# Batch 0 of a fused attention and feed-forward kernel: two of three head groups over all queries at once, undivided plain columns, and a finer first cast

## The chip, the cores and the metric

The kernel runs on one core of a Trainium2 chip. The metric is the device time of one execution in microseconds (us), the median of the runs shown. The engines are named as in the profile: PE (TensorE, the matrix unit; PEld its weight loads), ACT (ScalarE), DVE (VectorE), POOL (GpSimd, which here issues most loads), SP (SyncE, which issues stores and the transposing loads).

## The reference

Two stages follow one another: attention with a squared ReLU in place of softmax, and a feed-forward pair with an exact GELU.

```python
scores = scale * np.matmul(q, k.transpose(0, 1, 3, 2))   # q, k, v: (8, 12, 448, 64) float32
attn = np.maximum(scores, 0.0) ** 2 / S
attn_out = np.matmul(attn, v)
x = attn_out.transpose(0, 2, 1, 3).reshape(B * S, H * D) # (3584, 768)
h = x @ w_in                                             # w_in: (768, 2048)
g = 0.5 * h * (1.0 + erf(h * inv_sqrt2))
return g @ w_out                                         # w_out: (2048, 768)
```

## The kernel before

All products run in bfloat16. There are eight batches; a batch has three head groups of four heads (G = 3), and 448 keys in seven blocks of 64 (NK = 7).

**Attention.** For one head group, `add_tk` and `add_tq` turn k and q on PE (tiles `tp`) and copy them out to `kT` and `qT`; from batch 2 on, transposing loads do this instead. `add_steps` makes one *step* out of one or two key blocks: the scores on PE into a PSUM tile `ps` (line 806), the scaled ReLU on ACT or DVE into a tile `a_sq` (lines 823, 825), the square on DVE or ACT (lines 835, 833). A step with all 448 queries holds one key block; where queries come in two halves of 224, a step holds two blocks of one half, so that both kinds give `a_sq` the same 896 columns. `add_av` multiplies the seven squared blocks with v (tile `pav`, line 885) and two copies put the result into `xT`, the input of the feed-forward stage (lines 548 and 550, which serve every copy and cast).

In batch 0 before the change, all three groups are cut into halves of queries: `halves(0)` takes the seven blocks of group 0, half 0, then the rest, half 1 last. Batches 1 to 7 take all queries at once, by `steps(b)`.

**Feed-forward.** Of the first layer's sixteen columns of 128 features, batch 0 computes eight directly: `add_f1`, tile `psh`, line 947, with a GELU on ACT (line 957). These are called plain columns here. They need `xT` of all three head groups. Before the change each plain `psh` tile holds two feature columns over half of the queries; the tiles of half 0 come first, so they need no attention of half 1. All else in the first layer, and the second layer, uses a seven-product block scheme (Winograd's), with tiles `pe` and `pb` (lines 1103, 1256) for the first layer and `pso` (line 1432) for the second.

**Order.** Nothing is scheduled at run time. Every operation is an `Op` in a list; the table `ORDER` names them one by one with their engine (P and Q for PE, where Q takes the other kind of PSUM bank; A for ACT, D for DVE, G for POOL, S for SP; Z is a filler matmul), and the instructions of each engine are issued in that order. `HOMES` gives each tile its buffer: "w" three PSUM tiles of two banks, "f" two of one bank, "a" fourteen `a_sq` buffers. An engine works strictly down its list: what waits holds up all that stands behind it on that engine.

**The start.** The first parts of k and q (tiles `k32`, `q32`; group 0) come as float32 by loads on ACT and SP, and are cast by `early`; all other loads are issued by POOL, in their order, with at most eight under way. Nine matmuls on zeros (`spin`) run ahead of the first transposes. The cast of k is cut at `K_CUT` = 4 blocks of seven; q32 holds the first two of four chunks of q.

Of the kernel before, what the change touches and what calls it, by code (L numbers as in the profile page):

```python
# [12 lines left out]
B, H, S, D = 8, 12, 448, 64  # L13
# [71 lines left out]
0120120120120121210210210201201201201201201201202012010021210011021201201201021012102021021200221121  # L85
2201201201200120210210202020010212002102102102102121011001121010201012012012012010110011220112012012
021211000101201210212012021
""".replace("\n", ""),
    "f": """
0101010101010101011010101011010101010101011011010101010010101010101010101010101010101001010100110101  # L90
01010
""".replace("\n", ""),
    "a": """
0123456789abcd32105649c8b297301a546d89c723b14605ada8c91734526d0a918b652c74301abd98c6b2a50419d3879483
d174725ac60b893d271064ba53c893c210a74d3a89a37405628bc14d29a8564db03718078313d710b52a8c49670532d20985
7b137987357398a06c14d2a7359b57b259aa760814cd39b264513c807ba
# [3 lines left out]
D16 G3 G2 Q17 D18 A13 P14 D15 A19 Q20 D21 P22 D23 P45 D46 P42 A43 P39 G4 G7 P24 A40 D25 P32 D33 P36  # L100
D37 P57 A58 Z1024 Q51 A52 Q28 D41 D29 D44 Q34 D35 D59 A47 G10 Q30 A31 P54 A55 G6 P26 D27 P99 P84 A85
Z672 P69 A70 Q72 D38 D53 D56 P60 A61 D100 D62 D71 A73 G5 P48 A49 P66 D50 A67 D68 P114 A115 Q87 A88
G121 P78 A79 D116 D74 P96 D97 G8 P63 A64 G9 Q75 A65 A76 A77 P93 D94 P111 P105 A106 D112 D113 D80
D107 A95 G11 P144 A145 P108 A109 P81 A82 A83 G120 Q132 P134 D133 G12 P146 A147 D135 P167 A168 P161
A162 D86 D89 D110 P179 D180 D98 D101 P148 A149 P90 A91 D92 G129 P173 A174 D169 G125 G124 Q136 D137
Q164 A165 P102 A103 A104 D175 P117 D118 A119 P170 D171 D172 D253 P138 A139 D163 D166 D181 D254 P176
A177 D178 P245 A246 P194 A195 P185 A186 D187 P200 G123 G128 A201 P150 A151 P249 A250 P197 D198 D199
P188 A189 P191 A192 P142 P140 P203 A204 D141 G122 P182 D143 P209 A210 A183 D205 D193 D196 P215 A216
A184 P247 A248 P251 A252 P212 A213 P221 A222 G127 G126 D190 D202 P206 A207 A208 Q224 G131 P261 P278
D257 D258 P218 A279 D255 D225 A262 A219 G152 G153 Q227 A228 P268 P285 A269 D256 P264 P281 D214 A282  # L110
A265 P263 P280 D223 A211 D217 D259 P273 D260 P270 P287 G130 A220 D226 D229 D266 D286 D288 A289 Q230
A231 A232 D271 P276 P293 D283 D274 A277 A294 D374 P290 D375 D377 P378 D291 P395 A396 A379 P380 P385
P402 A275 A386 A403 A284 D376 D412 D415 P397 D400 D383 A272 P381 P398 D413 A382 P407 A399 D408 P416
P433 D434 A401 P404 P390 G240 G241 D450 P387 D391 A292 A384 D388 D405 A417 A392 A409 P419 P436 A437
A389 P423 P440 A420 A441 D414 G243 D453 D457 P410 A267 D458 P393 A411 A394 S233 P425 P442 D443 S234
Q302 A424 D426 P314 A315 A427 A303 P445 P428 P431 D429 A430 P418 D446 D451 D459 A432 Q308 A309 A444
P317 A318 P435 D438 D421 D454 P448 A449 D456 D460 D319 P462 A463 P305 A306 P311 P320 A321 A322 P464
A316 D465 P466 P468 D452 D304 D461 G155 G156 G158 G159 G239 A312 A467 S236 S235 P329 A406 A330 A313
P341 A342 D469 D455 P335 D336 D310 D307 A439 P470 D471 P472 P326 D327 S238 A447 A422 D494 S237 P368
A369 P350 A351 D495 P474 D475 P362 G242 G154 P323 G157 G160 A363 D473 D324 P344 D328 D352 A345 D346  # L120
A325 A337 D331 D496 P353 A354 D355 D497 P498 A499 P500 D501 P338 A339 D340 D343 P359 P332 A333 D334
G244 G295 G296 G297 S478 S476 A364 A360 A370 P502 D503 P504 D505 P356 A361 P347 A348 A349 D357 A358
P365 D366 D367 P506 D507 S479 P532 P523 A524 P526 D527 A533 P508 P514 D515 D516 D525 P520 A521 P371
A372 A373 D586 P529 P517 A518 A530 P510 D528 P590 A522 P607 A608 D587 D589 P597 D511 D531 P592 P614
A615 D591 D588 P609 D595 A596 G298 P593 P619 D612 P610 P626 A598 D624 P602 A611 D620 A594 P643 A627
A534 A644 G299 G300 G484 S481 S482 S483 S477 A613 D603 A604 A621 P616 P599 D617 D600 A601 P628 P645
D648 D631 D509 A618 P629 A632 D630 P622 D625 P605 P633 P650 D651 A623 A606 P646 P635 A634 S480 P547
Q538 A539 D676 A548 P655 P638 D636 D647 D519 D639 A640 P641 P652 P556 D656 A657 A557 D653 P544 D545
G487 G301 Q535 G490 G485 G486 D536 P568 G488 G489 G491 G492 A642 A654 P541 A542 D677 P658 A659 D540
D537 P680 D681 A569 A549 D678 D543 S662 D570 P565 D566 S512 P574 A575 P553 A554 A555 P682 P684 D683  # L130
A685 P550 A551 S660 S513 P562 P577 A563 A578 A649 A637 S663 S661 G666 G669 P686 D546 D558 D552 P688
D687 D689 P580 D581 P571 G493 P559 A572 A576 A560 P716 P734 A735 A561 P690 D679 P692 D579 D717 D696
D697 A567 A564 A718 D691 D699 D693 S695 P728 P722 A729 P719 A720 A723 P700 D701 P702 D721 D573 A582
P704 P740 A741 D703 P731 D732 D705 A724 P583 A584 A585 P749 D750 A736 P725 A726 A727 P708 P792 P809
D698 P794 P706 P811 D788 D733 D751 D742 D789 P799 P816 A817 A810 D730 D707 D709 P712 A793 D800 P710
D814 D791 P795 A796 D713 A815 D797 A798 P804 D711 P821 D805 P812 D813 P752 D822 A753 Q737 P743 A744
P755 A756 A757 D790 P801 P818 D819 P828 P845 A829 A823 A846 A738 A739 P830 D802 P824 P847 D826 D827
P831 P848 D850 D833 A851 A803 D832 D849 S665 S664 Q764 G672 G667 G668 G670 P835 P852 P837 P854 G671
G673 G674 A825 A806 A765 A745 P807 A808 D836 D853 D838 D855 A856 P840 P857 D841 A839 A842 D878 D858
D879 D880 P843 P860 A844 A861 P882 A859 A883 P746 A747 P773 P770 D771 D772 D766 S715 S862 S714 S864  # L140
S865 P884 D885 A774 D775 P758 S866 S863 P933 P930 A931 D754 P886 D887 A748 D934 G868 G871 G675 P888
P890 D889 D881 A834 A820 A759 D898 D891 P892 D893 S896 P927 D928 D929 P779 A935 A760 A780 D781 P761
A762 A763 P782 D783 P767 D900 D899 P902 A903 P894 D895 D932 A768 D769 A784 P776 A777 P924 D925 D926
P954 A955 A778 S867 S694 G874 G869 G870 P906 P904 D905 P936 D937 P918 A919 G872 G873 G875 A938 G876
P785 D786 D787 P921 A922 D901 P948 P908 A907 P945 A946 D992 D909 A923 P960 A956 A961 A949 P910 D911
D990 P912 P914 D920 D913 D991 D915 P994 A995 D950 P942 A943 A944 Q966 D967 P939 P957 A958 Q951 P1011
D993 P997 S1067 P1001 P1018 A1002 A1019 S916 S1065 G1070 G1073 S1064 S1066 S897 G877 D940 D941 D998
P996 D1012 P1013 D1016 D999 A1000 P1014 D1015 P1023 P1006 D1007 P1030 P1047 P1003 A1008 A968 D1024
A1025 P1032 D1048 P1049 D1028 D1052 A1031 A959 D1035 A1036 P1020 D1021 P1033 P1050 A1051 A1034 A1017
D1004 D1029 D952 D953 P1037 P1054 P1026 A1053 A1055 P1039 P1056 A1038 D1040 D1057 P1009 A1010 A1058  # L150
A1027 P1042 P1059 A1005 D1043 D1060 P1045 P1062 A1046 A1063 A1044 A1041 P1084 A1085 D1080 P969 P978
A979 D1082 P984 A985 D1081 P1086 D970 P1088 D1083 D1087 P1090 A962 A1061 A947 D1091 P972 P1138 A1139
A1022 D973 D974 D971 A986 P963 A1089 A980 P1135 A1136 P975 D964 D976 D965 P1094 D1095 P1092 D1093
P981 A982 P1144 A1145 P1126 A1127 D1100 D1101 D1137 D983 P1104 P1096 D1097 S1099 P1153 D1154 A977
P1159 A1160 P987 A988 A989 P1123 D1124 P1150 A1151 P1106 D1105 P1132 A1133 P1120 A1121 P1129 D1130
P1108 D1107 S917 D1122 D1152 D1102 D1103 D1109 D1161 A1140 A1134 A1155 P1196 P1198 P1215 P1213 A1197
D1201 A1214 P1110 S1069 G1076 S1068 S1098 G1071 G1072 P1112 D1111 D1218 A1219 D1113 A1125 D1192
D1193 P1114 G1074 G1075 G1077 D1115 D1131 D1194 A1128 P1116 D1117 P1162 A1163 D1146 P1141 A1142
D1195 P1168 D1169 Q1147 A1148 A1149 A1143 P1199 P1216 D1170 G1078 S1271 D1200 P1203 P1220 Q1186
D1217 P1156 A1204 A1221 A1187 A1157 P1222 P1205 D1230 D1164 D1206 A1202 D1223 A1224 P1225 P1208  # L160
D1209 A1210 D1226 P1232 P1249 D1250 P1228 D1231 P1234 P1251 A1233 A1188 D1237 D1254 P1235 P1252
A1229 D1253 P1211 P1239 P1256 A1227 A1238 A1255 A1212 D1236 P1241 P1258 D1240 D1242 A1158 A1207
A1257 D1259 A1243 P1180 D1181 A1260 Q1174 A1175 P1244 P1261 P1247 D1262 A1263 P1264 A1265 A1248
# [1607 lines left out]
```

## Time and profile before

| | |
|---|---|
| median of 3 runs | 357.82 us (357.68 to 358.1) |
| profiled execution | 357.81 us, its span 356.0 us |
| granted PE clock | 1.000 |
| busy: PE, ACT, DVE, POOL | 98%, 76%, 86%, 29% of the span |
| matmuls | 3853 |

The span runs from the first to the last instruction of the execution; 1.8 us of its time lie outside. A row of the timeline reads: start, duration, engine, line, operation, output and input, shape, count, and in brackets the idle time ahead of it on that engine and what ended it. Consecutive instructions of one kind stand in one row, and its shape is that of the first of them. Durations overlap at their ends: what an instruction costs its engine's queue is the distance from its start to the next one's.

### The profile page before, as it was taken

How to read it: one execution, taken by the hardware profiler on the slowest of the kernel's cores; microseconds unless marked ns; L12 is line 12 of the kernel's file. 1: busy time of each engine (PE TensorE's matmuls, PEld its weight loads, DVE VectorE, ACT ScalarE, POOL GpSimd, SP SyncE). 2: the span in 40 equal slices, each digit the busy share in tenths (PEclk: the TensorE clock that was granted, in tenths of full speed). 3: DMA queues.
4: the chain of work that ended last, by engine and by line, in shares of the span. 5: the costliest groups of instructions: out<-in, count | busy, mean ns of one | idle time of the engine just before them, and what ended most of it. 6: DMA issues, size and time to landing. Idle time of an engine off the chain costs nothing.

```text
span 356.0 us, 9239 instructions
## 1 busy us (share of the span) xinstructions
PE 348.8 (98%) x3853; PEld 249.7 (70%) x3853; DVE 305.4 (86%) x514; ACT 269.0 (76%) x442; POOL 103.3 (29%) x138
## 2 busy tenths in 40 slices
PE   8899999999999999999999999999999999999995
PEld 4577689855589556786557965669669856888663
DVE  4999999999989998779988979898998799588662
ACT  4999987999978999498787798879986896412500
POOL 8665814195346102901093100290001000000000
PEclk9999999999999999999999999999999999999999
DMA  9999999999999956997699900799309103020222
GB/s 172 200 203 204 184 184 183 162 153 149 200 154 113 184 79 98 124 181 94 132 117 176 175 2 0 186 119 168 37 2 182 22 0 129 8 89 2 88 90 88
DMA packets 123465, 43.01 MB, mean 121 GB/s; under 512 B 100896, under 2 KB 120096, under 8 KB 123424
## 3 DMA queue, kind: packets, MB, share of 16 engines
q0 software_dynamic: 84432, 22.47, 66.9%
q1 hardware_dynamic: 38448, 19.50, 26.0%
q8 instruction: 30, 0.49, 0.6%
q10 hardware_dynamic: 544, 0.46, 0.4%
q14 instruction: 11, 0.09, 0.1%
HBM read 45.61 MB, written 11.01 MB: 159 GB/s over the span
## 4 chain that ended last, share of the span: by engine, by line
PE 93%; ACT 4%; DMA 1%; DVE 1%; issue 0%; DVEq 0%
PE pso L1432 37%; PE pe L1103 30%; PE ps L806 10%; PE pav L885 9%; PE pb L1256 5%; ACT a_sq L823 3%; PE psh L947 2%; DMA k<-in_k_dram 1%; ACT a_sq L833 1%; PE tp L667 0%; PE tp L696 0%; ACT h_sb L957 0%; DVE kT L548 0%; DVE nk L548 0%; ACT xT L550 0%
## 5 line engine op out<-in xcount | busy, mean ns | idle before, releaser
L823 ACT ACTIVATE a_sq<-ps 128x896 bf16<-128x896 f32 (+1 forms) x135 | 108.3, 863 | 9.7 <-PE ps L806 9.6
L1432 PEld LDWEIGHTS <-s_sb 128*128 128x128 bf16 x456 | 43.0, 98 | 31.5 <-issue 4.3
L835 DVE TENSOR_TENSOR a_sq<-a_sq 128x896 bf16<-128x896 bf16 x106 | 61.7, 617 | 1.7 <-ACT a_sq L823 1.0
L1103 PEld LDWEIGHTS <-win_sb 128*128 128x128 bf16 x624 | 59.2, 98 | 3.7 <-issue 2.8
L833 ACT ACTIVATE a_sq<-a_sq 128x896 bf16<-128x896 bf16 (+1 forms) x63 | 58.2, 950 | 0.9 <-DVE a_sq L825 0.6
L825 DVE TENSOR_SCALAR a_sq<-ps 128x896 bf16<-128x896 f32 (+1 forms) x51 | 50.6, 1003 | 3.4 <-PE ps L806 2.8
L1141 DVE TENSOR_TENSOR part<-pe,part 128x448 f32<-128x448 f32 x78 | 45.3, 619 | 8.0 <-PE pe L1103 7.3
L806 PE MATMUL ps<-qT,kT 64*64 64x448 bf16 (+1 forms) x756 | 49.1, 337 | 1.2 <-ACT a_sq L823 0.6
L1153 ACT ACTIVATE h_sb<-part 128x448 bf16<-128x448 f32 x78 | 42.6, 579 | 8.4 <-DVE part L1141 7.9
L1432 PEld LDWEIGHTS <-h_sb 128*128 128x128 bf16 x336 | 31.7, 98 | 23.4 <-issue 4.8
L1103 PEld LDWEIGHTS <-ws 128*128 128x128 bf16 x468 | 44.5, 98 | 2.1 <-issue 1.1
L1432 PE MATMUL pso<-wout_sb,h_sb 128*128 128x384 bf16 x224 | 41.1, 326 | 0.0
L1432 PE MATMUL pso<-t_sb,s_sb 128*128 128x384 bf16 x224 | 41.1, 326 | 0.0
L1432 PE MATMUL pso<-wout_sb,s_sb 128*128 128x384 bf16 (+2 forms) x232 | 41.0, 321 | 0.0
L588 POOL DMA_DIRECT2D nk<-in_k_dram x36 | 34.7, 969 | 11.3 <-DMA kT<-nk 5.1
L885 PE MATMUL pav<-a_sq,v_sb 64*64 64x448 bf16 (+1 forms) x756 | 36.3, 329 | 0.5 <-ACT a_sq L823 0.4
L550 ACT COPY part<-pe 128x448 f32<-128x448 f32 x52 | 26.0, 539 | 14.0 <-PE pe L1103 10.1
L806 PEld LDWEIGHTS <-kT 64*64 64x64 bf16 x756 | 19.7, 105 | 21.7 <-issue 15.2
L1103 PE MATMUL pe<-t_x,win_sb 128*128 128x224 bf16 x312 | 34.8, 259 | 0.0
L1103 PE MATMUL pe<-xT,win_sb 128*128 128x224 bf16 x312 | 34.5, 259 | 0.0
L1103 PE MATMUL pe<-t_x,ws 128*128 128x224 bf16 x312 | 34.0, 259 | 0.0
L506 POOL DMA_DIRECT2D nq<-in_q_dram x36 | 30.0, 838 | 10.8 <-DMA wout_sb<-in_moe_w_out_dram 10.3
(73 smaller groups left out, 399.3 us busy)
## 6 DMA issues: line engine op xcount, KB each, us to landing
out_dram<-osb SPq DMA_DIRECT2D x19, 384.0 KB, 2.9
nq<-in_q_dram POOLq DMA_DIRECT2D x37, 112.0 KB, 5.8
nk<-in_k_dram POOLq DMA_DIRECT2D x36, 112.0 KB, 5.0
v_sb<-in_v_dram POOLq DMA_DIRECT2D x5, 672.0 KB, 7.9
v_sb<-in_v_dram POOLq DMA_DIRECT2D x9, 224.0 KB, 7.1
win_sb<-in_moe_w_in_dram POOLq DMA_DIRECT2D x8, 192.0 KB, 9.2
wout_sb<-in_moe_w_out_dram POOLq DMA_DIRECT2D x1, 1536.0 KB, 15.2
wout_sb<-in_moe_w_out_dram POOLq DMA_DIRECT2D x4, 384.0 KB, 18.7
```

Of the source, the lines that this page charges most:

```text
L506: nc.gpsimd.dma_start(nq[b][:, g0, :, e], rows)
L588: nc.gpsimd.dma_start(nk[b][:, g0, :, e], rows[:, e].rearrange("p (i d) -> p i d", d=D))
L806: nc.tensor.matmul(side(ps, e)[64 * j : 64 * j + 64, x * w : x * w + w], kT[r, g, i * 128 + 64 * j : i * 128 + 64 * j + 64], moving, start ...
L823: A.activation(to, x, AF.Relu, scale=c_att)
L825: V.tensor_scalar(to, x, c_att, 0.0, op0=mybir.AluOpType.mult, op1=mybir.AluOpType.max,)
L833: A.activation(ar, ar, AF.Square)
L835: V.tensor_mul(ar, ar, ar)
L885: nc.tensor.matmul(side(pav[0], e)[o2 : o2 + 64, :w], vt[b][r, 2 * g + e, bass.ts(i, D)], box["a2"][r, e, o : o + w], start=(i == 0), stop ...
L1103: nc.tensor.matmul(bank[name][:, y, z * HS : z * HS + HS], w[:, k, bass.ts(mm, 128)], right()[:, k], start=first and k == 0 and z == 0, st ...
L1141: V.tensor_add(get(to), ps(name), get(other))
L1153: A.activation(h_ring()[:, m : m + 2, o + half[c].start : o + half[c].stop], src().rearrange("p (x n) -> p x n", x=2), AF.Gelu,)
L1432: nc.tensor.matmul(box[bank][:, n0:n1], left()[:, kf], right()[:, kf, n0:n1], start=bool(need) and kf == 0, stop=kf == K2 - 1, skip_group_ ...
```

## The change

Four things change in the code, and the order table with them.

1. In batch 0, only head group 0 is still cut into halves of queries (seven steps of two blocks); groups 1 and 2 take `steps(0)`, all queries at once, fourteen steps of one block. `add_tq` turns four chunks of q at once for them.
2. The eight plain columns are computed undivided: one column over all 448 queries in a `psh` tile.
3. The first cast of q is done in two chunks, of k in three pieces (two blocks, two, three), and the k pieces are turned as they come. DVE or ACT may take each; the table decides.
4. `HOMES` and `ORDER` are written anew for all engines and the whole program. All line numbers from 1041 on, and those of functions below the table, fall by one.

```diff
 HOMES = {
...
-0120120120120121210210210201201201201201201201201202012010021210011021201201201021012102021021200221121
...
 ORDER = """
-D16 G3 G2 Q17 D18 A13 P14 D15 A19 Q20 D21 P22 D23 P45 D46 P42 A43 P39 G4 G7 P24 A40 D25 P32 D33 P36
...
-    PLAIN = [(m + x, h) for m in HALF_M for x in range(2) for h in range(2)]
+    PLAIN = [(m + x, None) for m in HALF_M for x in range(2)]
...
-        d = 0.34 if eng == "DVE" else 0.093 + n / 1200
-        return sch.add(((eng, d, d + 0.13),), fn, [landed(t)])
-
-    o = early("ACT", lambda: nq[0][:, :4, : HC * D], q32, 4.72)
+        d = 0.064 + n / 960, 0.093 + n / 1200
+        both = (("DVE", d[0], d[0] + 0.13), ("ACT", d[1], d[1] + 0.13))
+        return sch.add(both, fn, [landed(t)])
+
     for c in range(HC):
-        ld_q[0, 0, c] = o
+        cc = slice(c * D, c * D + D)
+        ld_q[0, 0, c] = early(
+            "ACT", lambda cc=cc: nq[0][:, :4, cc], q32[:, :, cc], 5.1
+        )
     add_tq(0, 0, 0, HC)
     ld_k[0, 0] = []
-    for eng, i0, i1, t in (("DVE", 0, K_CUT, 4.55), ("ACT", K_CUT, NK, 5.04)):
+    for eng, i0, i1, t in (("DVE", 0, 2, 4.85), ("DVE", 2, K_CUT, 4.85), ("ACT", K_CUT, NK, 5.4)):
         c = slice(i0 * D, i1 * D)
         o = early(eng, lambda c=c: nk[0][:, :2, c], k32[:, :, c], t)
         ld_k[0, 0] += [o] * (i1 - i0)
         add_tk(0, 0, i0, i1)
+    add_tq(0, 0, HC, NC, T_LATE)
     for g in (1, 2):
         add_tk(0, g)
-        add_tq(0, g, 0, HC)
-    for g in range(G):
-        add_tq(0, g, HC, NC, T_LATE)
-    st0 = halves(0)
-    add_steps(st0[:11], dve=True)
-    add_steps(st0[11:], HALF_BIAS, True)
+        add_tq(0, g)
+    x = [(0, 0, i, half) for half in range(2) for i in range(NK)]
+    add_steps([tuple(x[n : n + 2]) for n in range(0, 2 * NK, 2)], dve=True)
+    add_steps(steps(0)[NK:], HALF_BIAS, True)
...
-    for m in HALF_M:
-        add_f1(0, m, 0, bias=F1_BIAS)
...
     for m in HALF_M:
-        add_f1(0, m, 1, bias=F1B_BIAS)
+        for y in range(2):
+            add_f1(0, m + y, bias=F1B_BIAS)
```

The numbers in the new lines are costs for a planner that the table overrides; they set nothing.

**The first casts, on ACT.** Ahead of these rows ACT has issued its two loads of k. Before:

```order
L550 CAST nq<-q_91 112x4x128 [waits DMAHW1_49]
L550 CAST nk<-k_92 128x2x192 [waits DMAHW2_49]
L823 ACTIVATE a_sq<-ps 128x896 [waits PE_49] x3
L823 ACTIVATE a_sq<-ps 128x448 [waits PE_49] x2
L833 ACTIVATE a_sq<-a_sq 128x2x224 [waits DVE_49]
```

After:

```order
L549 CAST nk<-k_92 128x2x128 [waits DMAHW0_49]
L549 CAST nq<-q_91 112x4x64 [waits DMAHW1_49]
L549 CAST nk<-k_92 128x2x128
L549 CAST nk<-k_92 128x2x192 [waits DMAHW2_49]
L549 COPY qT<-tp 128x2x224 [waits PE_49]
L822 ACTIVATE a_sq<-ps 128x896 [waits PE_49] x2
```

ACT now casts all of k and half of q, and copies a turned q out ahead of its first ReLU; DVE, which cast the first part of k, casts the other half of q.

**The loads, on POOL.** The rows follow POOL's first load and its making of the identity matrix (that first load was `nk` of head group 1, and is now the second half of group 0's q, half as large). Before:

```order
L501 DMA nq<-in_q_dram 112x4x256 x2
L501 DMA nq<-in_q_dram 112x4x128
L585 DMA nk<-in_k_dram 128x2x448
L608 DMA v_sb<-in_v_dram 128x2x448
L501 DMA nq<-in_q_dram 112x4x256
L608 DMA v_sb<-in_v_dram 128x2x448
L608 DMA v_sb<-in_v_dram 128x2x448 [waits DMASW0_49]
L521 DMA win_sb<-in_moe_w_in_dram 128x3x256 [waits DMASW1_49]
```

After:

```order
L584 DMA nk<-in_k_dram 128x2x448
L500 DMA nq<-in_q_dram 112x4x256 x2
L584 DMA nk<-in_k_dram 128x2x448 x2
L607 DMA v_sb<-in_v_dram 128x2x448
L584 DMA nk<-in_k_dram 128x2x448
L500 DMA nq<-in_q_dram 112x4x256 [waits DMASW0_49]
L500 DMA nq<-in_q_dram 112x4x256 [waits DMASW1_49]
L520 DMA win_sb<-in_moe_w_in_dram 128x3x256 [waits DMASW2_49]
L521 DMA win_sb<-in_moe_w_in_dram 64x3x256 [waits DMASW3_49]
L522 DMA win_sb<-in_moe_w_in_dram 64x3x256 [waits DMASW4_49]
L607 DMA v_sb<-in_v_dram 128x2x448 [waits DMASW5_49]
L607 DMA v_sb<-in_v_dram 128x2x448 [waits DMASW6_49]
```

The loads of v move back: group 0's from the sixth to the seventh place, those of groups 1 and 2 from the eighth and ninth behind two loads for batch 1 and the first weights.

**The first plain columns, seen on ACT.** `h_sb<-psh` is the GELU of one plain tile, `xT<-pav` a copy of finished attention. Before:

```order
L550 CAST xT<-pav 128x224 [waits PE_49] x2
L823 ACTIVATE a_sq<-ps 128x896 [waits DVE_49,PE_49]
L833 ACTIVATE a_sq<-a_sq 128x896 [waits DVE_49,Activation_49]
L957 ACTIVATE h_sb<-psh 128x2x224 [waits PE_49]
L823 ACTIVATE a_sq<-ps 128x896 [waits PE_49] x2
L833 ACTIVATE a_sq<-a_sq 128x896 [waits Activation_49]
L957 ACTIVATE h_sb<-psh 128x2x224 [waits PE_49]
```

After:

```order
L549 CAST xT<-pav 128x448 [waits PE_49] x2
L822 ACTIVATE a_sq<-ps 128x896 [waits PE_49] x2
L822 ACTIVATE a_sq<-ps 128x896 [waits DVE_49,PE_49]
L956 ACTIVATE h_sb<-psh 128x448
L822 ACTIVATE a_sq<-ps 128x896 [waits DVE_49,PE_49]
L956 ACTIVATE h_sb<-psh 128x448 [waits PE_49]
L822 ACTIVATE a_sq<-ps 128x896 [waits DVE_49,PE_49]
```

Before, the first GELU follows the copies of half 0 and 19 steps' scores on PE; after, it follows the copies of the whole batch 0 and 27 steps' scores.

More of the change, by code (lines that the diff above doesn't have):

```diff
@@ L105 @@
[L105 to L114, printed above, removed]
@@ L185 @@
[L185 to L187 removed]
+D14 G10 G2 A17 Q18 D19 A13 P15 D16 P26 A20 Q21 D22 A23 Q24 D25 P36 A27 Q51 D52 A37 D38 P42 P57 A58
+D59 A43 P39 A40 G3 P28 D29 G4 P30 D31 P54 P45 A46 D55 Z1024 D53 D47 Q69 A70 D71 P66 A67 D56 P75 A76
+P81 A82 Z672 G7 P34 P78 G6 G115 A79 P32 G5 G111 G112 D35 D33 P60 A61 P72 A73 D41 D44 D62 D68 Q87 A88
@@ L188 @@
+D1555 D1557 D1525 P1558 D1559 S1562 S1281 A1523 A1520 A1492 A1543 A1540 A1526 D1564 D1565 P1560
+D1561 S1563 P1568 D1567 D1566 P1570 A1569 P1572 D1571 A1573 P1574 P1576 D1575 D1577 P1578 D1584
+D1579 D1585 P1580 D1581 S1583 S1582 D1586 P1588 P1590 D1587 A1589 P1592 D1591 A1593 S1604 P1594
+P1596 D1595 D1597 S1605 P1598 D1599 S1606 P1601 P1600 D1603 S1608 D1602 S1607
 """
```

173 lines of the change are left out of this document (88 added, 85 removed).

## Prediction

> **What bounds the kernel now.** I read the page's first parts, then busy time by stage, then the chain of waits, then the opening in order of time. PE is busy for 98% of the span, at full clock in every slice, and the stages tell where it is not:
>
> ```profile
> span 356.0 us, 9239 instructions
> ...
> PEclk9999999999999999999999999999999999999999
> ...
> 10.00:20.00 10.00, 8.52 (x230) 5.81 (x224) 9.42 (x18) 10.00 (x21) 6.55 (x10) 1.00 1.32 201
> 30.00:40.00 10.00, 10.00 (x170) 7.10 (x160) 9.65 (x18) 9.20 (x14) 7.09 (x10) 1.00 1.47 195
> ```
>
> The columns of a stage are its length, then the busy time of PE, PEld, DVE, ACT, POOL, then clock, DMA share and GB/s. From 10 to 20 us ACT is full (10.00) and DVE nearly (9.42), while PE waits; from 30 us on PE is full. So the kernel has an opening bound by ACT and DVE, which do batch 0's ReLUs and squares, and a long stretch bound by PE. The chain shows where one hands over to the other (start, length, what):
>
> ```profile
> 25.06 0.44 ACT h_sb L957
> 25.54 1.31 PE psh L947 x12
> 26.85 0.80 PE pav L885 x28
> ...
> 28.66 1.49 PE pav L885 x56
> ...
> 32.42 0.69 PE ps L806 x12
> 33.11 2.41 PE psh L947 x24
> ...
> 36.21 0.51 PE tp L696 x16
> 36.73 0.39 PE tp L667 x14
> ...
> 43.56 0.19 PE ps L806 x4
> ...
> 71.46 1.30 PE pso L1432 x8
> ...
> 352.45 0.29 DVE osb L1466
> ```
>
> From 25.54, the third plain tile, to 352.45 PE never leaves the chain: 326.91 us. The prediction is therefore a sum of two: when PE becomes the bound in the changed kernel (call it T), and what work PE then still has.
>
> **The work that is left.** In the new order all of batch 0's attention, 27 steps' scores and the transposes of five head groups' k and q stand ahead of the first plain column. So T is the start of that column, and what lies behind it, against what lay behind 25.54, is counted from the two orders:
>
> - eight undivided columns (48 matmuls of 448) instead of six half tiles (72 of 224). Two half tiles took 2.41 with one mode switch, 1.15 each. A 448-wide one of this kind has no row; by the 384-wide row it is 1.30/8 x 448/384 = 0.190, six 1.14, and it can hardly exceed two half ones, 1.15. I take 1.14: 9.12 - 6.90 = +2.22.
> - three products with v over half the queries gone: -(0.80 + 1.49) = -2.29.
> - three steps' scores gone: -3 x 0.19 = -0.57.
> - one turn of k, one of q gone: -(0.39 + 0.41) = -0.80, the 0.51 row less 0.1 for its switch.
> - three changes between attention and feed-forward fewer (105 to 102). The twelve scores' row, 0.69 against 3 x 0.19, prices one at 0.12: -0.36.
>
> Sum -1.80. PE ends at T + 325.11; at T = 27.34 nothing would change.
>
> [...]
>
> The undivided scores and products with v in groups 1 and 2 save PE more: 112 matmuls. That lies ahead of T, where PE waits for ACT, and I cost it at nothing; the cover is ACT's queue below. Without that cover it would be a gain.
>
> **T, from ACT's queue.** The rows of the opening:
>
> ```profile
> 4.92 0.59 DVE L548 CAST nk<-k 128x512 bf16<-128x512 f32 x1 [3.90 <-DMA k<-in_k_dram]
> 5.20 0.62 ACT L550 CAST nq<-q 112x512 bf16<-112x512 f32 x1 [1.93 <-DMA q<-in_q_dram]
> 5.57 0.41 PE L667 MATMUL tp<-ident,nk 128*64 128x128 bf16 x8 [0.55 <-DVE nk L548]
> 5.72 0.51 ACT L550 CAST nk<-k 128x384 bf16<-128x384 f32 x1
> 5.87 0.39 PE L696 MATMUL tp<-ident,nq 112*64 112x112 bf16 x8
> 6.28 0.75 PE L667 MATMUL tp<-ident,nk 128*64 128x128 bf16 x20
> 7.09 0.67 PE L806 MATMUL ps<-qT,kT 64*64 64x224 bf16 x20
> 7.63 3.41 ACT L823 ACTIVATE a_sq<-ps 128x896 bf16<-128x896 f32 x5 [1.40 <-PE ps L806]
> 11.76 4.28 ACT L823 ACTIVATE a_sq<-ps 128x896 bf16<-128x896 f32 x6
> 11.94 0.62 DVE L548 COPY kT<-tp 128x896 bf16<-128x896 bf16 x1
> 12.47 1.69 DVE L835 TENSOR_TENSOR a_sq<-a_sq 128x896 bf16<-128x896 bf16 x3
> 14.07 1.09 DVE L825 TENSOR_SCALAR a_sq<-ps 128x896 bf16<-128x896 f32 x1
> 15.80 0.47 ACT L550 CAST xT<-pav 128x224 bf16<-128x224 f32 x1
> 16.03 3.19 ACT L823 ACTIVATE a_sq<-ps 128x896 bf16<-128x896 f32 x5
> 30.89 0.91 ACT L550 COPY qT<-tp 128x896 bf16<-128x896 bf16 x1
> 31.70 0.92 ACT L823 ACTIVATE a_sq<-ps 128x896 bf16<-128x896 f32 x1
> 32.93 2.56 ACT L823 ACTIVATE a_sq<-ps 128x896 bf16<-128x896 f32 x3
> 35.32 1.04 ACT L957 ACTIVATE h_sb<-psh 128x448 bf16<-128x448 f32 x2
> 36.16 2.62 ACT L823 ACTIVATE a_sq<-ps 128x896 bf16<-128x896 f32 x3
> 40.01 0.53 ACT L550 CAST xT<-pav 128x448 bf16<-128x448 f32 x1
> 40.42 0.94 ACT L823 ACTIVATE a_sq<-ps 128x896 bf16<-128x896 f32 x1
> ```
>
> *The first ReLU.* A 512-column cast on ACT lasts 0.62 and a 384 one 0.51, so a 256 one 0.40, and the next starts 0.10 before its end. ACT casts k from 4.92, q's first chunk from 5.22, k again from 5.52 and 5.82, until 6.33; DVE has q's second chunk by 5.6. PE turns the first k blocks at 5.37, q from 5.67 to 6.06 (eight in 0.39), then the eight chunks loaded by POOL to 6.45, then ten of k at 0.05 each to 6.95. The first PE score row carries twelve matmuls before the ReLU at 7.63, 0.042 each, so eight take 0.33 and ACT starts at 7.28, 0.35 earlier than now. POOL's load must have landed by 6.06; its first load, twice as large, was being turned within the row that starts at 6.28. So the start is late by 0 to 0.4; half the bytes in the same place, I take 0. The second step that ACT takes is PE's fourth, ready at 6.95 + 4 x 0.33 = 8.27, while ACT is free at 8.08: 0.2 lost.
>
> *What it then does.* Up to the copies of batch 0's last attention the new order has on ACT 19 wide ReLUs, six narrow ones, two narrow copies, one turned q and two wide copies of attention. Wide ReLU: (35.32 - 32.93)/3 = 0.797. Narrow (of the six at 11.76 four are wide): (4.04 - 4 x 0.797)/2 = 0.43. Narrow copy 0.23, turned q 31.70 - 30.89 = 0.81, wide copy 40.42 - 40.01 = 0.41. Sum 15.14 + 2.58 + 0.46 + 0.81 + 0.82 = 19.81. From 7.28 + 0.2 that ends at 27.29. The last copy counts to its visible end, 0.12 later, and PE follows 0.05 after: T = 27.46.
>
> *DVE beside it.* From about 7.6 its list up to its own copies of that attention has 21 squares at (14.07 - 12.47)/3 = 0.53, two ReLUs at 1.0, six turned tiles at 12.47 - 11.94 = 0.53, and four copies of attention, at most 0.53: 18.4, so 26.0. That is 1.3 us before ACT: cover, not bound.
>
> *Loads.* POOL's rows show landings, since a row waits for the load eight before it:
>
> ```profile
> 11.94 0.75 POOL L521 DMA_DIRECT2D win_sb<-in_moe_w_in_dram  x1 [0.43 <-DMA v_sb<-in_v_dram]
> 14.21 0.63 POOL L522 DMA_DIRECT2D win_sb<-in_moe_w_in_dram  x1 [1.53 <-DMA nq<-in_q_dram]
> 28.55 0.73 POOL L608 DMA_DIRECT2D v_sb<-in_v_dram  x1 [1.11 <-DMA win_sb<-in_moe_w_in_dram]
> ```
>
> In units of one head group's k, 5.5 had landed at 11.9 and 19.5 at 28.5: 1.19 us a unit. Now group 0's v is the seventh load, 6.5 units, as the nq that landed by 14.21; ACT wants the copy of its product at about 15.5, and the product takes 0.86 at most, so 0.4 is spare. Group 1's v (12.25 units) comes near 20.0, its product's slot at 21.7; the weights for the sixth column (25 units) near 35.1, needed at 36.5. All hidden, by 0.4 to 1.7 us.
>
> **Sum.** 27.46 + 325.11 = 352.57 against 352.45: +0.12 on the profiled 357.81, so 357.93, and since the profiled run is 0.01 from the median I give 357.9: no change that a measurement can tell, which for this kernel takes about 0.2%, 0.7 us.
>
> **Rivals.**
>
> *ACT stays the bound past T (slower).* Between the copies and the third column ACT must do four wide ReLUs and two GELUs (0.42 by the rows at 35.32): 4.03, to 31.4 with the handover. PE gets there after two columns, six steps, a turn of q and five switches: 2.28 + 1.14 + 0.41 + 0.6 = 4.4, at 31.9. Some 0.4 is spare. Before, ACT lost as much in one go in this region:
>
> ```profile
> 30.62 0.35 ACT L550 CAST xT<-pav 128x224 bf16<-128x224 f32 x1 [0.40 <-DVE xT L548]
> ```
>
> A loss ahead of T moves T whole; one past it counts beyond the 0.4 spare. Three losses of 0.4 ahead of T give 359.1; from 0.6 on the result is slower. Against it: in the row at 11.76 ACT runs six ReLUs without a stop. Chance 0.24.
>
> *A load is late (slower).* If group 0's v or the sixth column's weights land 1.5 to 2 us after my line, PE stands for 1.1 or 0.6: 358.5 to 359.0. It decides from 1.1 us of lateness at v. Chance 0.07.
>
> *The clock falls (slower).* The granted clock is full in every slice, though PE waits in the opening. If the new order's longer opening cost it half its clock from 11 to 27 us, some 10 us of PE work there would take 20 in 16.5: T 3.5 us later, 361.4. [...] Chance 0.01.
>
> *PE's long stretch holds waits that the new order loses (faster).* Counted from the order and priced by the rows, what lies behind 25.54 is 1260 block-scheme matmuls of the first layer at (2.41 - 0.11)/24 = 0.0958, 776 of the second at 0.1625 and 16 narrower ones (1.3 in all), 1164 wide scores and products with v at 0.19/4, 10.8 for the half products, tiles and turns, and 105 switches at 0.11: 325.7. Measured are 326.91. The 1.2 between is the most that an order can win back; 0.7 of it, with T on its line, gives 357.2. An earlier T alone does not do it: were all early PE work at the later rates (14 turns of k 0.39, scores 0.034), the first ReLU would come 0.4 sooner and the 0.2 not be lost, T = 26.9 and 357.3. Both in part reach 357.0. Against it: the scheme behind T is the same, and its 1.2 may be no waits at all. Chance 0.18.
>
> *The change doesn't do what it says.* The orders show that it does.
>
> **Numbers.** Within 0.2%: 0.50 (forecast). Slower: 0.24 + 0.07 + 0.01 = 0.32. Faster: 0.18. The range goes from the faster case, 357.0, to three losses, 359.1; beyond lie about 1 in 10 on each side.
>
> **What would show it.** First ReLU at 7.3 (right) or after 7.6; no ACT wait over 0.2 up to 27 us; first `psh` at 27.2 to 27.7; PE in the chain without a break from there; 3693 matmuls, and 325.1 us from the first `psh` to PE's end. A wait of PE for `a_sq` or `h_sb` between 27 and 36 us, or for `win_sb` or `v_sb`, makes it wrong to the slow side; a first `psh` before 26.7 to the fast one.

## The result, and the profile after

| | before | after |
|---|---|---|
| median of four runs each | 357.75 us (357.57 to 358.1) | 362.75 us (361.52 to 363.63) |
| profiled execution, its span | 357.81, 356.0 us | 362.94, 360.8 us |
| ratio, 95% interval | | 1.0130 (1.0103 to 1.0158) |

The changed kernel is 1.3% slower, against a forecast of 357.9 and a range up to 359.1. Its runs also differ more: by 2.1 us, against 0.5 before. Ratios leave disturbed runs out, of which there were some in experiments 1 and 2, while the medians hold all runs.

What follows explains the profiled run, the only one of the four with a trace. Its mean PE clock is 0.993; in the other three runs it is 0.998, 0.998 and 1.000, and the longest of all, 363.63, is the one at 1.000.

The page of the changed kernel, its head and the row of PE's clock:

```profile
span 360.8 us, 8923 instructions
...
PEclk9999999899999999999999999999999999999999
```

In the eighth of 40 slices (63 to 72 us) the clock is below full, far behind the opening. The stages (columns as in the prediction):

```profile
10.00:20.00 10.00, 8.78 (x188) 5.36 (x188) 9.95 (x19) 10.00 (x17) 6.35 (x10) 1.00 1.34 199
30.00:40.00 10.00, 10.00 (x94) 4.90 (x96) 9.22 (x18) 8.33 (x14) 6.41 (x9) 1.00 1.28 201
66.00:69.00 3.00, 3.00 (x18) 2.37 (x17) 2.53 (x5) 1.10 (x3) 0.00 (x0) 0.50 1.75 132
```

Up to 20 us ACT is full, and from 30 PE is, as forecast. From 66 to 69 PE is full too, but at half clock: 18 matmuls in 3 us. The timeline of the changed kernel around that place, first on PE:

```profile
62.31 1.31 PE L1102 MATMUL pe<-t_x,ws 128*128 128x224 bf16 x12
65.61 2.20 PE L1102 MATMUL pe<-t_x,ws 128*128 128x224 bf16 x12 [1.99 <-DVE part L1140]
67.61 3.27 PE L1102 MATMUL pe<-t_x,win_sb 128*128 128x224 bf16 x24
```

Twelve such matmuls last 1.31, and 24 last 2.46 at full clock (undisturbed rows of the same kind stand in experiment 4). Here they take 2.20 and 3.27, so 0.89 + 0.81 = 1.70 us go to the clock, behind a wait of 1.99. What PE waited for stands in the timeline of DVE:

```profile
60.78 0.62 DVE L547 COPY part<-pe 128x448 f32<-128x448 f32 x1
64.06 0.96 DVE L1365 TENSOR_TENSOR t_sb<-wout_sb 128x1536 bf16<-128x1536 bf16 x1 [2.65 <-DMA wout_sb<-in_moe_w_out_dram]
64.94 1.68 DVE L1140 TENSOR_TENSOR part<-pe,part 128x448 f32<-128x448 f32 x3
```

DVE's next instruction at 61.4 is a sum of second-layer weights (`t_sb`, from the output weights `wout_sb`) that DVE takes up again only at 72.6 us and PE at 75.7. It waits 2.65 us for a load, and behind it on the same engine stand three additions that empty PE's tiles `pe`. They are ready, and PE, which stands from 63.62, needs the first of them. DVE does not pass the sum over: it starts at 64.06, and the additions at 64.94, right behind it. Why the load was late is in the chain of waits and in POOL's timeline:

```profile
43.51 20.53 DMA wout_sb<-in_moe_w_out_dram
64.04 0.02 issue
64.06 0.04 DVE t_sb L1365
64.10 0.84 issue
64.94 0.63 DVE part L1140
```

```profile
53.86 0.98 POOL L587 DMA_DIRECT2D nk<-in_k_dram  x1 [3.14 <-DMA nk<-in_k_dram]
57.38 0.84 POOL L505 DMA_DIRECT2D nq<-in_q_dram  x1 [2.54 <-DMA nk<-in_k_dram]
64.32 0.82 POOL L505 DMA_DIRECT2D nq<-in_q_dram  x1 [6.10 <-DMA wout_sb<-in_moe_w_out_dram]
...
73.48 0.20 POOL L769 COPY gate<-qT 128x16 bf16<-128x16 bf16 x1 [8.12 <-DMA qT<-nq]
...
79.49 1.41 POOL L760 COPY gate<-qT 128x16 bf16<-128x16 bf16 x1 [3.38 <-DMA qT<-nq]
```

Each of the load rows goes on when the load eight before it has landed, the one at 53.86 behind a landing at 53.58. Two halves of batch 2's second k land by 53.6 and 57.1, 3.5 us apart, while packets of SP's transposes of batch 2 move (47.0 to 56.6); the large weight load, now behind them, lands at 64.04. Before, it stood ahead of them and landed at 53.98, the same waits ended earlier, and the sum ran at once:

```profile
54.26 0.82 POOL L506 DMA_DIRECT2D nq<-in_q_dram  x1 [8.14 <-DMA wout_sb<-in_moe_w_out_dram]
...
73.28 0.72 POOL L761 COPY gate<-qT 128x16 bf16<-128x16 bf16 x1
```

```profile
60.98 0.95 DVE L1366 TENSOR_TENSOR t_sb<-wout_sb 128x1536 bf16<-128x1536 bf16 x1
```

The new table also moved two other things on the DMA side: batch 1's last v stands ahead of batch 2's first k and q, and SP turns batch 2's third k ahead of its third q. POOL's gate that waits for that q, ahead of all loads of batch 3, started at 73.28 before and at 79.49 now.

### The profile page after: what moved, and what is told of

The parts are those of the page before. It is cut to its first block, busy times and chain, and to the rows that moved or that the text cites. A ratio compares the mean times of both kernels' runs of the same rounds, so it can differ in the third digit from the quotient of the medians.

```text
span 360.8 us, 8923 instructions
## 1 busy us (share of the span) xinstructions
PE 350.7 (97%) x3693; PEld 245.2 (68%) x3693; DVE 304.3 (84%) x511; ACT 268.4 (74%) x440; POOL 103.7 (29%) x138
## 4 chain that ended last, share of the span: by engine, by line
PE 81%; DMA 15%; POOL 2%; issue 1%; DVE 0%; DVEq 0%; POOLq 0%
PE pso L1431 36%; PE pe L1102 25%; PE ps L805 8%; DMA v_sb<-in_v_dram 7%; PE pav L884 7%; DMA wout_sb<-in_moe_w_out_dram 6%; PE pb L1255 4%; DMA nk<-in_k_dram 2%; POOL nq L500 1%; POOL nk L584 1%; POOL nk L587 1%; DVE part L1140 0%; DVEq L1766 0%; POOL ident L1553 0%; DVE osb L1465 0%
## 5 line engine op out<-in xcount | busy, mean ns | idle before, releaser
L834 DVE TENSOR_TENSOR a_sq<-a_sq 128x896 bf16<-128x896 bf16 x111 | 65.5, 618 | 1.7 <-ACT a_sq L822 1.5
L824 DVE TENSOR_SCALAR a_sq<-ps 128x896 bf16<-128x896 f32 (+1 forms) x55 | 52.4, 966 | 2.7 <-PE ps L805 2.6
L832 ACT ACTIVATE a_sq<-a_sq 128x896 bf16<-128x896 bf16 x57 | 52.9, 958 | 0.8 <-DVE a_sq L824 0.5
L1152 ACT ACTIVATE h_sb<-part 128x448 bf16<-128x448 f32 x78 | 43.4, 585 | 4.2 <-DVE part L1140 4.2
L549 ACT COPY part<-pe 128x448 f32<-128x448 f32 x54 | 27.5, 539 | 15.9 <-PE pe L1102 9.8
L1465 DVE TENSOR_TENSOR osb<-pso,p_sb 128x384 f32<-128x384 f32 x42 | 23.3, 554 | 14.9 <-PE pso L1431 13.0
```

The lines of the kernel that those rows point to most:

```text
L549: A.copy(dst, src)
L824: V.tensor_scalar(to, x, c_att, 0.0, op0=mybir.AluOpType.mult, op1=mybir.AluOpType.max,)
L832: A.activation(ar, ar, AF.Square)
L834: V.tensor_mul(ar, ar, ar)
L1152: A.activation(h_ring()[:, m : m + 2, o + half[c].start : o + half[c].stop], src().rearrange("p (x n) -> p x n", x=2), AF.Gelu,)
```

## The experiments

Each kernel was timed beside the kernel before on the same chip, whose medians lay between 357.82 and 357.92. Two kinds of names in the diffs: `D441` is the sum of output weights, `D382 D379 D396` the three additions; `G224 G223 G226` load the first small, the large and the last small output weights, `G138` loads batch 2's second k, `S220` and `S221` turn its third k and q, `G121` loads batch 1's last v, `G135 G136` batch 2's first k and q. In the kernel before the same loads are `G241 G240 G243`, `G155`, `G130` and `G152 G153`, the transposes `S237 S238`.

**1. The sum behind the additions.**

```diff
-G223 D441 A392 A377 P381 D382 A408 D379 D396
+G223 A392 A377 P381 D382 A408 D379 D396 D441
```

> After the change, with one instruction moved on VectorE: the first sum of output weights (t_sb from wout_sb), which waited 2.7 us for a load with three part additions queued behind it, now stands behind those three additions. Theory (the wait in the queue is the cause): PE's wait of 1.99 us at 63.6 us and the 3.3 us at half clock behind it both go; together they held PE up by 2.15 + 1.67 = 3.8 us, so 362.9 - 3.8 = 359.1 us, PE clock 1.00 in every slice. Rival (the additions are only the last of several late things, and PE next waits for another): at most 1 us is won, 361.9 or more. Rival (the loss lies all over the long stretch): no change, 362.7.

Measured: 361.06 us, ratio 1.0074 (1.0061 to 1.0087), six runs from 360.14 to 369.68. In the trace the wait at 64 us and the half clock are gone, but not 3.8 us. In the profiled run (362.92) PE stands later, for a transposed q of batch 3; waits of PE in the long stretch, then the place in PE's timeline:

```profile
PE ps L805 <- DMA qT<-nq: 2.9, 1, 2.9
PE pe L1102 <- DVE part L1140: 0.6, 1, 0.6
```

```profile
98.58 0.76 PE L805 MATMUL ps<-qT,kT 64*64 64x448 bf16 x12 [2.88 <-DMA qT<-nq]
```

So the first cause is real and hid a second: the DMA side runs late past this load too, and the wait at 64 us had kept PE from meeting the next late transfer. In the changed kernel PE comes to these scores at 98.64, just behind the q that lands at 98.34; here it is ready at 95.70, and the q lands at 98.45. In the kernel before that q landed at 92.21.

**2. k behind the output weights.**

```diff
-G224 G138 P369 P386
+G224 P369 P386
...
-P401 G226 D444
+P401 G226 G138 D444
```

> After the change, with one load moved on POOL's queue: the two halves of batch 2's second k group, which stand ahead of the large output-weight load, now stand behind all output-weight loads, and VectorE's order is untouched. Theory (the sum of output weights is late because these 0.45 MB were put ahead of the large load while transposes share the DMA engines, each half taking 3.5 to 4 us to land): the large load lands near 57 instead of 64.04, the sum waits for nothing, 359.1 us. Rival (the transposes on SP set when the weights land, in whatever order they are issued): the load still lands after 62, 362 or more. Rival (k is now late for its own transpose): the sum is in time, but the gates and batch 2's scores wait, over 360.

Measured: 363.76 us, ratio 1.0117 (1.0077 to 1.0158), six runs from 360.13 to 367.35. The profiled one is the best, 360.13. There the load does what the theory says, if later: it lands at 60.19, not near 57, the sum waits for nothing, and PE waits 0.36 in all. The time is still 1.0 above the 359.1 forecast, about what the work behind T was misjudged by (see below). POOL's timeline, at the wait that this load ends:

```profile
60.47 0.98 POOL L587 DMA_DIRECT2D nk<-in_k_dram  x1 [8.94 <-DMA wout_sb<-in_moe_w_out_dram]
```

The other runs were not profiled. That they lose 1 to 7 us more is not explained by this run. The three longest show a mean clock of 0.989 to 0.993, so the clock fell there too; the place near 96 us, where PE waits its 0.36 for a transposed q, is one candidate for what they waited for.

**3. The kernel before, with k ahead of the large weights.**

```diff
-G240 G241 D450
+G241 G155 G240 D450
...
-G155 G156 G158
+G156 G158
```

> The kernel before, with its output-weight loads and batch 2's second k group issued in the order of the changed kernel (the two small weight loads, k, the large load, the two small ones); its opening, its plain columns and VectorE's order are untouched. Theory (the order of the loads alone makes the loss): the large load lands near 65 instead of 53.98, the sum at 60.98 waits some 4 us, the additions behind it come late, PE waits 2 to 3 us and its clock halves for some 3.4 us: 361.5 to 363 us. Rival (the loss comes from the new opening and the undivided columns, and the loads are hidden): 357.8.

Measured: 358.07 us, ratio 1.0015 (0.9999 to 1.0032), one run of eleven at 361.5. The rival is nearer. The large load does land late, at 62.64, 8.7 us later than in the kernel before, and in the profiled run (359.41) the sum waits 1.51 and PE 0.85. That is less than the theory wanted, and most runs lose less still: one moved load is not enough.

**4. The gap filled.**

```diff
-A428 P414
+A428 Z4320 P414
...
+    zero0 = zero
...
         def fn(e):
+            zero = zero0 if n in (1024, 672) else ident
```

(The diff is written with the operation numbers of the changed kernel.)

> After the change, with nine matmuls of 64x480 or so on constants (4320 columns, 1.8 us, their result is not used) put on PE ahead of the matmul that waits 1.99 us for the part addition. Theory (the clock halves because PE stood idle for 2 us): the additions are as late as before, but PE is never idle for over 0.3 us there, the clock stays 1.00, and the 1.67 us lost at half clock are won: 361.3 us. Rival (the clock falls for another reason at that place, or the fill doesn't count as work): clock still 0.5 from 66 to 69 us, 362.7 to 363.0.

Measured: 361.94 us, ratio 1.0110 (1.0097 to 1.0123), runs within 0.2. PE's timeline:

```profile
63.75 2.02 PE L1579 MATMUL fill<-ident 64*64 64x512 bf16 x9
65.93 1.31 PE L1102 MATMUL pe<-t_x,ws 128*128 128x224 bf16 x12 [0.16 <-DVE part L1140]
67.08 2.46 PE L1102 MATMUL pe<-t_x,win_sb 128*128 128x224 bf16 x24
```

The additions are as late as before, the clock stays full, and the same rows that took 2.20 and 3.27 take 1.31 and 2.46. With PE idle for 0.16 us in place of 1.99 the clock did not fall; in all four runs of this kernel its mean is 1.000. The time is 0.6 above the theory's 361.3: in the profiled run the load lands 0.32 later than in the changed kernel's, and PE waits 0.35 for a transposed q at 97.3.

**5. Half of the gap filled** (`Z2160` in place of `Z4320`).

> After the change, with matmuls on constants for 0.9 us (2160 columns, their result is not used) ahead of the matmul that waits for the part addition, so that PE idles some 1.0 us instead of 1.99. The full fill gave 361.9 us and a full clock, no fill 362.7 and half a clock for 3.3 us. Theory A (the clock falls when the busy share over a window of a few us falls too low, so an idle 2 us was enough and 1 us is not): clock 1.00, 361.9 us. Theory B (any idle stretch over some 0.8 us halves it): half clock for 3.3 us, 362.7 us or more.

Measured: 361.51 us, ratio 1.0102 (1.0089 to 1.0115); PE waits 0.79 and runs on at full clock. Theory B is out, and the result is what theory A said.

**6. The sum and the transposes.** Experiment 1, and on SP:

```diff
-S220 D464 A430 D485 D304 D310 D486 D334 D487 P320 A321 D322 P323 A319 A324 S221
+S221 S220 D464 A430 D485 D304 D310 D486 D334 D487 P320 A321 D322 P323 A319 A324
```

> After the change, with the sum moved behind the three additions as in the first experiment, and on SP's queue the last two transposes of batch 2 in the order of the kernel before: third q ahead of third k. Theory (the second loss is the third q: POOL's second gate waits for it, to 79.4 us, and every load of batch 3 stands behind that gate; before, the gate opened at 73.3): the gate opens near 75, batch 3's first q lands near 94 instead of 98.4, PE's wait of 2.88 us at 95.7 goes, 362.9 - 2.9 = 360.0 us for the run that the first experiment's profile showed, and runs within 0.5 of each other. Rival (the transposes are slow because the DMA engines are full, and the order only shifts who waits): PE still waits 2 us or more near 96, 361 or more, runs spread by 1 us or more.

Measured: 360.46 us, ratio 1.0070 (1.0055 to 1.0084), runs 1.5 apart. No wait near 96 us: the gate opens at 77.7, and batch 3's first q lands at 96.2, later than I wrote and early enough. PE waits 0.96 at 70.2 instead, for an addition. The spread of 0.5 that the theory gave did not come.

**7. All loads as before.** Experiment 6, with the loads of 33 us and later in the old order:

```diff
-G121 Q213
+G135 G136 G121 Q213
...
-G135 G136 G224 G138 P369
+G223 G224 P369
...
-P378 G223
+P378
...
-P401 G226 D444
+P401 G226 G138 D444
```

> After the change, with the sum and the transposes as in the experiment beside it, and POOL's loads from 33 us on in the order of the kernel before: batch 2's first k and q ahead of batch 1's last v, the large output-weight load ahead of the small ones, batch 2's second k behind them all. Theory (all that was lost behind the first plain column came from the order of loads, sums and transposes): no PE wait over 0.4 us behind 28 us, clock 1.00 throughout, large weights landed by 55, batch 3's first q by 93; PE ends 326.2 us behind the first plain column as in the second experiment's profile, 27.7 + 326.0 + 3.6 + 2.1 = 359.4 us, runs within 0.5. It stays 0.4% slower than before, since the sum of work behind that column was 0.8 to 1.0 too low. Rival (the forecast's sum was right and 326.2 still holds hidden waits): 358.5. Rival (the new opening makes the DMA stream late by itself): waits stay, 361 or more.

Measured: 360.36 us, ratio 1.0068 (1.0056 to 1.0080), five runs within 0.4. The spread of experiment 6 is gone, and only loads were moved against it. It is 1 us above the theory: 0.58 of it is one wait of PE at 69.6 for an addition.

**8. The kernel before, with all three DMA moves of the change.**

```diff
-G152 G153 Q227
+G130 G152 G153 Q227
...
-G240 G241 D450
+G241 G155 G240 D450
...
-S238 A447 A422 D494 S237
+A447 A422 D494 S237 S238
```

> The kernel before with only its DMA order changed, to that of the changed kernel: batch 1's last v ahead of batch 2's first k and q, batch 2's second k ahead of the large output-weight load, third k ahead of third q on SP. Opening, plain columns, VectorE and PE order untouched. Theory (three moved transfers add up: 1.1 us for v, then the 0.8 us PE gap of the experiment with k alone grows by the same 1.1 and halves the clock, and the third q delays batch 3): PE idles 1.5 to 2 us near 64 with its clock at half behind it, or near 96: 361 to 362.5 us, runs spread by 1 us or more. Rival (it takes the new opening as well): 358.0 to 358.6, as k alone gave.

Measured: 359.28 us, ratio 1.0039 (1.0027 to 1.0051), five runs within 0.3. PE waits 0.94 at 63.3 and keeps its clock; the sum waited for the same load:

```profile
62.66 0.96 DVE L1366 TENSOR_TENSOR t_sb<-wout_sb 128x1536 bf16<-128x1536 bf16 x1 [1.61 <-DMA wout_sb<-in_moe_w_out_dram]
```

On the kernel before, the moves alone cost 1.4 us; the theory's 3 to 4.6 were too much. In the changed kernel the large load lands at 64.04 against 62.64 here; there PE waits 1.99, and the clock falls.

**9. Loads and transposes as before, the sum where the change put it.** Experiment 7 without the move of `D441`.

> After the change with POOL's loads and SP's transposes in the order of the kernel before, as in the experiment that repaired everything (360.36), but with the sum of output weights left where the change put it, ahead of the three part additions. Theory (the sum is harmless as soon as its weights have landed: VectorE idles 1.2 us just there, and moving the sum behind the additions only pushed it into a full stretch and made PE's 0.58 us wait at 69.6): the large load lands near 55, the sum runs at 61.6 without waiting, no PE wait behind 28 us, 359.8 us. Rival (the sum itself, late or not, holds the additions up): PE waits 0.4 us or more near 64, 360.4 or more.

Measured: 359.84 us, ratio 1.0057 (1.0041 to 1.0073), five of six runs within 0.3 and one at 360.90. No PE wait in the long stretch; the sum runs at 61.69. The theory is right for this trace, and the 0.58 us of experiment 7 were made by moving the sum.

**10. Two transfers only.** The k of experiment 2 and the third q of experiment 6, nothing else.

> After the change with two transfers moved back: batch 2's second k behind all output-weight loads, third q ahead of third k on SP; v's place, the order of the weight loads and VectorE as the change has them. Theory (these two are what counts, v and the order of the weights shift things by some 1 us that is hidden): the weights land near 60.2 as in the second experiment, just ahead of the sum at 61.4, batch 3's first q by 94: 359.8 to 360.1 us, runs within 0.5. Rival (without v's move everything on the DMA side runs 1.1 us late, and the margin is gone): runs spread by 1 us or more, median over 360.5.

Measured: 359.72 us, ratio 1.0047 (1.0035 to 1.0059), six runs from 359.5 to 359.82. The clock is full in every slice, and POOL's timeline shows both repairs, the large load ahead of 59.75 and the gate for the third q at 73.47:

```profile
59.75 0.98 POOL L587 DMA_DIRECT2D nk<-in_k_dram  x1 [8.82 <-DMA wout_sb<-in_moe_w_out_dram]
...
70.61 0.75 POOL L769 COPY gate<-qT 128x16 bf16<-128x16 bf16 x1 [5.92 <-DMA qT<-nq]
...
73.47 0.20 POOL L760 COPY gate<-qT 128x16 bf16<-128x16 bf16 x1
```

PE has no wait behind 27 us of over 0.2. Its first plain column and its last matmuls, the ends of the stretch that is compared below:

```profile
27.88 1.31 PE L946 MATMUL psh<-xT,win_sb 128*128 128x448 bf16 x6
...
352.56 1.48 PE L1431 MATMUL pso<-wout_sb,s_sb 128*128 128x128 bf16 x16
```

**11. The third q only.**

> After the change with one transfer moved back: third q ahead of third k on SP. With the second experiment (k alone, 363.8, runs 360.1 to 367.4) and the last one (both, 359.72, runs 359.5 to 359.8) this makes the square of the two. Theory (two separate losses, the first at 64 us from k ahead of the large weights, the second at 96 us from the third q): the first stays whole, the large load lands near 64, PE waits some 2 us for the additions: 361.4 to 362.9, depending on whether the clock falls, and no wait near 96. Rival (the third q is the whole cause, and the wait at 64 would vanish in its shadow): 360 or less.

Measured: 361.26 us, ratio 1.0097 (1.0084 to 1.0110), just under the theory's 361.4. The first loss stays, in its smaller form, and there is no wait near 96 us; PE's timeline:

```profile
65.12 1.31 PE L1102 MATMUL pe<-t_x,ws 128*128 128x224 bf16 x12 [1.04 <-DVE part L1140]
66.26 2.46 PE L1102 MATMUL pe<-t_x,win_sb 128*128 128x224 bf16 x24
```

The large load lands at 63.55, and a wait of 1.04 leaves the clock full. The four medians of the square: neither moved back 362.75, q alone 361.26, k alone 363.76, both 359.72. For k alone the median says little: three of its six runs, at a mean clock of 0.999 to 1.000, lie from 360.13 to 362.21, the other three, at 0.989 to 0.993, from 365.31 to 367.35, and only the best was traced. With q alone the first loss is seen to stay; that the second is what spoils k alone is likely, not shown. Only with both moved back are all runs short and close together.

**12. The changed kernel again.**

> The changed kernel once more, for a second trace of it. Theory (the loss is a race of loads against the queues, so it repeats in kind and differs in size): median 361.5 to 363.6, PE waits 1.5 to 3 us behind a part addition near 64 us with the large weight load landing near 64, in some runs with the clock at half behind it, or near 96 us for a transposed q. Rival (the wait at 64 us was an accident of the one trace): no wait there, or in another place.

Measured: 363.32 us, ratio 1.0143 (1.0112 to 1.0175), runs from 361.27 to 365.28. Three of the six show a mean clock of 0.994 or 0.995, the others 0.998 to 1.000, so the clock falls in some runs only. The profiled run (364.26) repeats the loss in the same place; PE's timeline, then its waits in the long stretch:

```profile
66.50 1.58 PE L1102 MATMUL pe<-t_x,ws 128*128 128x224 bf16 x12 [2.13 <-DVE part L1140]
67.88 3.89 PE L1102 MATMUL pe<-t_x,win_sb 128*128 128x224 bf16 x24
```

```profile
PE pe L1102 <- DVE part L1140: 2.1, 1, 2.1
PE ps L805 <- DMA qT<-nq: 0.4, 1, 0.4
```

## Why the prediction was wrong

**The step that failed is the paragraph on loads.** It followed POOL's queue up to the weights of the sixth plain column, needed at 36.5, called all of it hidden, and stopped. The order of loads had changed behind that point too, and the part of the kernel that I took as "PE in the chain without a break" rests on those loads. The rival "a load is late" had the right kind of cause, at the wrong places (group 0's v, the sixth column), at 0.6 to 1.1 us instead of about 3.5, and with a chance of 0.07. What was missing in it is the step from the load to PE: PE's first matmul with output weights starts at 73.6, almost 10 us behind the late load, but an early sum waits for it ahead of three additions that PE needs. None of the prediction's signs of being wrong, a wait for `a_sq`, `h_sb`, `win_sb` or `v_sb`, names this one.

From forecast to measurement, in the profiled execution:

| term | forecast | measured | difference |
|---|---|---|---|
| T, first plain column | 27.46 | 27.51 | +0.05 |
| PE's work behind T, no waits (experiment 10) | 325.11 | 326.17 | +1.06 |
| wait and half clock (329.70 behind T here, less 326.17) | 0 | 3.53 | +3.53 |
| time outside the span | 1.8 | 2.1 | +0.3 |

Together 4.97 of the 5.0 between 357.93 and 362.94, with 0.33 for the last row. The rows of the timeline gave 1.99 + 1.70 = 3.69 for the third.

**T came out right, in part by luck.** The timeline of ACT, its first ReLUs and the copies of batch 0's last attention, and that of PE:

```profile
7.00 8.27 ACT L822 ACTIVATE a_sq<-ps 128x896 bf16<-128x896 f32 x11 [0.23 <-PE ps L805]
...
26.41 0.97 ACT L549 CAST xT<-pav 128x448 bf16<-128x448 f32 x2
```

```profile
27.51 1.31 PE L946 MATMUL psh<-xT,win_sb 128*128 128x448 bf16 x6
```

The first ReLU starts at 7.00 (forecast 7.28), the column at 27.51. The two are 20.51 us apart where the forecast had 20.18: an early start made up for a list on ACT that was costed 0.33 too low. Over the eleven traces with this opening the ReLU starts between 6.89 and 7.66, the two are 20.50 to 21.08 apart, and T lies between 27.51 and 28.26, so the forecast is at the low end: 0.4 below T in experiment 10. One wait of the opening was not foreseen, 0.73 us of PE for a load of q at 15.9; ACT was busy through it.

**The work behind T was too low by 1.06.** PE's last matmuls before, and in the changed kernel:

```profile
350.93 1.48 PE L1432 MATMUL pso<-wout_sb,s_sb 128*128 128x256 bf16 x16
```

```profile
355.72 1.48 PE L1431 MATMUL pso<-wout_sb,s_sb 128*128 128x128 bf16 x16
```

Against the 326.87 of before (25.54 to 352.41), experiment 10 saves 0.70, where the sum had 1.80. By kind: the undivided columns +2.19 (forecast +2.22), so 0.19 us a matmul was right; products with v -2.06 (-2.29); turns of k and q -0.91 (-0.80); scores and switches together -0.31 (-0.57 - 0.36), since the trace has two switches fewer, 104 to 102, not three, and one second-layer group more ends in one; and +0.4 on block-scheme matmuls whose count did not change. Without any wait the changed kernel is therefore slower too, by some 0.5% (experiments 9 and 10): with this work T had to come near 26, and it did not.

**The rivals.** *ACT stays the bound past T*: no; in none of the eleven traces has PE a wait for ACT of over 0.2 us behind T. *PE's long stretch holds waits that the new order loses*: no; with no wait left it still takes 326.17, and before PE had no wait of over 0.2 us behind 25.54 either, so the 1.2 us between count and measurement are not such waits. *The clock falls*: it did in the profiled run, but not in the opening that I priced: it fell behind a wait that a load made. Its chance of 0.01 was my estimate: no run had shown which waits cost the clock. Here waits of 1.99 and 2.13 us were enough, while 2.88 us in experiment 1 left the clock full: the length of one wait does not tell. The half clock lasted 3.41 us here (65.85 to 69.26) and 3.42 in experiment 12 (67.40 to 70.82).

The traces say more. The record of the granted clock in the changed kernel's trace begins at 4.41 us, and its changes, at 65.85, 69.26 and 359.40, lie 18, 19 and 104 steps of 3.413 us behind that. In the trace of the kernel before it begins at 4.92, and its one change, at 356.49, lies 103 such steps behind. Counted by these steps, the two falls of the changed kernel's trace come at the end of steps in which PE stood still for 1.99 us (the wait) and 2.19 (the end of its work), and the fall in the kernel before at the end of a step behind its last matmul. In all steps ahead of these ends but that of the wait PE stood still for 1.01 us at most, and none of them ended in a fall. Stages cut at the steps, of the changed kernel and then of experiment 1 around its wait of 2.88 us:

```profile
62.44:65.85 3.41, 1.42 (x16) 1.26 (x14) 1.79 (x3) 1.49 (x4) 1.03 (x2) 1.00 1.74 182
65.85:69.26 3.41, 3.41 (x21) 2.69 (x19) 2.94 (x6) 1.36 (x4) 0.00 (x0) 0.50 1.72 130
```

```profile
93.95:97.37 3.42, 1.75 (x16) 0.70 (x8) 2.60 (x5) 2.30 (x3) 0.00 (x0) 1.00 2.33 180
97.37:100.78 3.41, 2.20 (x24) 1.12 (x28) 1.39 (x2) 1.58 (x2) 0.20 (x1) 1.00 1.23 196
```

The wait of 1.99 lies in one step, which leaves PE 1.42 us of work in it. The wait of 2.88 is divided at 97.37, into 1.67 and 1.21, and the clock is 1.00 in every us from 94 to 107: neither part was enough. How the steps lie to the work differs from run to run: in experiment 12 the wait ends 0.89 us later than in the changed kernel's first trace (66.50 against 65.61), the fall comes 1.55 later (67.40 against 65.85). So the same wait need not cost the clock in every run: by the mean clocks (0.993 to 0.995, against 0.998 to 1.000) it fell in four of the changed kernel's ten runs.

**What stays open.** Why the large load lands 1.4 us later in the changed kernel than in experiment 8, in the same order of loads from 33 us on; what the unprofiled runs of experiment 2 lost, and which waits the unprofiled runs of the changed kernel met, one of which (363.63) kept its clock; and the 0.3 us outside the span, which all runs with the new opening have (2.1 against 1.8).

## What to carry to other kernels

When a change rewrites the order of a whole program, follow each DMA queue to its end, not only to the place where the bound changes hands: list what every late load releases, and above all what stands behind the first instruction that waits for it on an in-order engine, needed or not. One repaired wait can uncover the next late transfer: with the 1.99 us at 64 repaired, PE waited 2.88 at 96 (experiment 1). One trace does not tell the spread: where the profiled run of experiment 2 had a PE wait of 0.36 us, its six runs lay 7.2 us apart. Here the fall of the clock behind a PE wait of 1.99 us cost 1.70 us more, and how the wait lay in the steps of the clock counted beside its length: one of 2.88, divided by a step into 1.67 and 1.21, cost no clock.

## What the runs showed of the hardware

- PE's clock fell to half for 3.4 us after waits of 1.99 and 2.13 us (the changed kernel, twice traced), and did not after waits of 0.58 to 1.04 (seven traces) nor after one of 2.88 (experiment 1). In the traces of the two kernels its changes lay whole numbers of steps of 3.413 us behind the first entry of the clock record (18, 19 and 104; 103). There, steps with 1.99, 2.19 and 3.41 us without matmuls ended in a fall, those with 1.01 or less did not; in experiment 1 neither did steps with 1.67 and 1.21. Filler matmuls on constants, which left PE waits of 0.16 and 0.79, kept it full (experiments 4 and 5).
- While packets of SP's transposes moved (47.0 to 56.6 us in the changed kernel's trace), half a k group took 3.5 us to land behind the one ahead of it (53.58 to 57.09); with none moving, a half took 0.7 us behind the load ahead of it (69.38 to 70.11).
